# Tile 1 of x loaded from GpSimd's queue, and K's fourth block of weights loaded from ScalarE's queue in its place

## The chip, the cores and the metric

The kernel runs on one core of one Trainium2 chip. The metric is the device time of one execution in microseconds (us); smaller is better. The kernel before takes 210.59 us (median of 3 runs, 210.23 to 210.78).

The engines are named as the profile names them: PE is TensorE (PEld its weight loads), DVE is VectorE, ACT is ScalarE, POOL is GpSimd and SP is SyncE, which here only issues DMAs. A name with a q behind it (SPq, ACTq) is the instruction stream of that engine where it issues a DMA.

## The reference

The input x has 2048 rows of 512 (bfloat16). It is normalised row by row, and two blocks are computed from the normalised rows and added to x:

```python
x  = A_x
xn = _layernorm(x, axis=-1)              # (x - mean) / sqrt(var + 1e-5)
return x + _A_ref(xn, A_wqkv, A_wo) + _B_ref(xn, B_w_gate, B_w_up, B_w_down)
# A: linear attention, 32 heads of 16; phi(t) = where(t > 0, t + 1, exp(t)) + 1e-6
#    q, k, v = xn @ wqkv; kv = phi(k)^T v, z = sum phi(k); out = (phi(q) kv) / (phi(q) z) @ wo
# B: (silu(xn @ w_gate) * (xn @ w_up)) @ w_down, hidden width 1792
```

## The kernel before

The rows are cut into 16 tiles of 128. A tile of x is a 128 KB load; a block of weights of K is 128 rows by 512 columns of `wqkv`, also 128 KB, and a projection of one tile needs four such blocks (0 to 3), one for each 128 of the 512 input features.

Nothing schedules the kernel: every operation is written into the list of one engine in the order of the source, and a small helper (`_Prog`) adds waits on semaphores by what each operation reads and writes. A DMA is one instruction in the list of the engine whose queue issues it, with a semaphore of its own. The helper's rules matter here: an operation that writes a tile waits for the last writer and for all the readers since, and a DMA that is given a tile in `after` counts as a reader of it until it has landed.

The start of the kernel is a chain through all engines, since there is nothing to multiply until the first tile of x has come in:

- PE first runs eight matmuls on constants (`fill(8, 512)`, L271), whose result nobody reads.
- SP issues, in this order: tile 0 of x, blocks 0 and 1 of K's weights (one DMA of 256 KB), block 2 of K's weights, tile 2 of x, two blocks of Q's weights, tile 3 of x, and so on.
- ACT issues two loads before its first work on data: tile 1 of x, which waits for the memset of `ident`, and then block 3 of K's weights, which waits for nothing.
- POOL clears `warm`, clears `ident` (L238), turns `ident` into the identity matrix by an affine select (L242) and sets `nhalf`. Because the load of tile 1 was given `ident` in `after`, the affine select waits until that load has landed.
- Tile 0: DVE takes mean and variance (L299, L302) and subtracts the mean in two halves (L382); PE transposes the halves with `ident` (L410); ACT copies them to `xcT` (L422).
- Tile 1: its mean is taken on ACT instead (`mean_act`, L307); then DVE, PE and ACT do the same as for tile 0.
- PE's list is: the fill; the transposes of tile 0 (first half, one small fill, second half); the two halves of tile 1; and then the projections (`proj_part`, L465), one matmul each. For tile 0 and K the blocks are taken in the order 0, 1, 3, 2; the same follows for tile 1, and then Q.

From there on come the projections of the other tiles (L452, L438), the sums over rows (L590), the feed-forward block (L785) and the output tiles (L979, L990), all on PE in the order of the source.

Of the kernel before, what the change touches and what calls it, by code (L numbers as in the profile page):

```python
# [109 lines left out]
def bass_parallel_sum__linear_attn_block__swiglu_ffn__prompt_kernel(  # L110
# [13 lines left out]
    pe, act, dve, pool, sp = nc.tensor, nc.scalar, nc.vector, nc.gpsimd, nc.sync  # L124
    bf, f32 = dt.bfloat16, dt.float32

    with contextlib.ExitStack() as es:
        E = es.enter_context

        def sb(name, shape, d=bf):  # L130
            return E(nc.sbuf_tensor(name, [P] + shape, d))
# [12 lines left out]
        ident = sb("ident", [P])  # L144
# [54 lines left out]
        def rows(v, t0, n):  # L199
            if t0 < NLONE:  # L200
                return v[t0 * P:(t0 + n) * P, :].rearrange("(t p) d -> p t d", p=P)
            return v[NLONE * P:, :].rearrange("(p t) d -> p t d", t=NT - NLONE)[:, t0 - NLONE:t0 - NLONE + n, :]

        def xload(eng, h, t0, n, after=()):
            K.dma(
                eng, lambda: h.dma_start(x_sb[:, t0:t0 + n, :], rows(xin, t0, n)),
                r=list(after), w=[("x", t0 + i) for i in range(n)],
            )

        def wqkv_load(eng, h, name, i, c0, n, after=()):  # L210
            K.dma(
                eng,
                lambda: h.dma_start(
                    wqkv_sb[:, c0:c0 + n, i * D:(i + 1) * D],
                    A_wqkv[c0 * P:(c0 + n) * P, i * D:(i + 1) * D].rearrange("(c p) f -> p c f", p=P),
                ),
                r=list(after), w=[(name, c) for c in range(c0, c0 + n)],
            )
# [14 lines left out]
            )  # L233

        K.op("pool", lambda: pool.memset(warm[:, :], 0.0), w=[("warm",)])
        K.op("act", lambda: act.activation(warm[:, :], warm[:, :], ACT.Exp), r=[("warm",)], w=[("warm",)])

        K.op("pool", lambda: pool.memset(ident[:, :], 0.0), w=[("ident",)])  # L238
        xload("act", act, 1, 1, [("ident",)])
        K.op(  # L240
            "pool",
            lambda: pool.affine_select(  # L242
# [6 lines left out]

        xload("sp", sp, 0, 1)  # L250
        wqkv_load("sp", sp, "wk", 1, 0, 2)
        wqkv_load("act", act, "wk", 1, 3, 1)
        wqkv_load("sp", sp, "wk", 1, 2, 1)
        xload("sp", sp, 2, 1)
        wqkv_load("sp", sp, "wq", 0, 0, 1)
# [832 lines left out]
```

## Time and profile before

| | us |
|---|---|
| time, median of 3 runs | 210.59 (210.23 to 210.78) |
| the profiled execution's own time | 210.51 |
| its span, first to last instruction | 209.3 |
| outside the span | 1.2 |
| PE busy | 206.6 (99%) |
| DVE, ACT, POOL busy | 120.2, 70.9, 72.0 |

In the profile, times are from the start of the span. A row of the timeline has the start, the length, the engine, the line, the operation, its tiles and how many instructions it merges; in brackets stands how long the engine was idle before it, and what released it. A row of the chain of waits has the start, the length and what ran. In a list of DMA issues the last number is the median time from issue to landing. Matmuls are pipelined: one of 512 columns is shown for about 0.38 us, but the next can start 0.22 us after it.

### The profile page before, as it was taken

The page shows a single profiled execution, that of the slowest core. Times are in us where ns is not written, and L with a number is a line of the kernel's source. Part 1 is how long each engine was busy: PE and PEld are TensorE (multiplying, and loading weights), DVE is VectorE, ACT ScalarE, POOL GpSimd, SP SyncE. Part 2 cuts the span into 40 slices and gives each one's busy share as a digit, 9 for nine tenths or more (in the row PEclk, how much of TensorE's full clock was granted, in tenths as well). Part 3 has the DMA queues.
Part 4 walks back from the last instruction along what each step waited for, and adds up shares of the span by engine and source line. Part 5 has one row for each costly group of instructions (what it writes and reads, how often), then busy time and mean ns, then how long its engine had stood idle before and what let it go on. Part 6 is the DMA issues. An engine that isn't in the chain of part 4 may idle for free.

```text
span 209.3 us, 2824 instructions
## 1 busy us (share of the span) xinstructions
PE 206.6 (99%) x1015; PEld 94.6 (45%) x1015; DVE 120.2 (57%) x246; ACT 70.9 (34%) x125; POOL 72.0 (34%) x90
## 2 busy tenths in 40 slices
PE   8999999999999999999999999999999999999996
PEld 3444444444444444444444444444444444444444
DVE  3999988336365874637355746365556545374122
ACT  5777666966643331312112312213031213121000
POOL 3427977568032543223041422240424132221200
PEclk9999999999999999999999999999999999999999
DMA  6673644894797011010101110102011010110101
GB/s 200 209 195 75 127 100 100 256 364 158 202 357 50 11 39 25 28 25 25 50 2 50 28 29 22 50 0 53 6 45 25 27 28 25 49 30 25 50 28 50
DMA packets 30287, 16.84 MB, mean 80 GB/s; under 512 B 20928, under 2 KB 29632, under 8 KB 30272
## 3 DMA queue, kind: packets, MB, share of 16 engines
q1 hardware_dynamic: 29984, 16.39, 29.9%
q10 hardware_dynamic: 288, 0.26, 0.4%
q8 instruction: 8, 0.13, 0.2%
q14 instruction: 7, 0.06, 0.1%
HBM read 9.70 MB, written 2.10 MB: 56 GB/s over the span
## 4 chain that ended last, share of the span: by engine, by line
PE 99%; DVE 0%; issue 0%
PE psum L785 46%; PE psum L990 23%; PE psum L438 10%; PE psum L979 7%; PE psum L590 7%; PE psum L271 2%; PE psum L465 2%; PE psum L452 2%; PE psum L410 1%; PE psum L892 0%; PE psum L915 0%; DVE out_sb L1003 0%
## 5 line engine op out<-in xcount | busy, mean ns | idle before, releaser
L800 ACT ACTIVATE sg<-psum 128x512 bf16<-128x512 f32 x56 | 33.4, 598 | 106.0 <-PE psum L785 102.5
L785 PE MATMUL psum<-xnT,wg_sb 128*128 128x512 bf16 x224 | 57.5, 379 | 0.0
L785 PE MATMUL psum<-xnT,wu_sb 128*128 128x512 bf16 x224 | 57.5, 379 | 0.0
L934 POOL TENSOR_TENSOR prod<-pkq,zb 128x512 f32<-128x512 bf16 x16 | 18.6, 1163 | 55.9 <-DVE pkq L514 55.9
L785 PEld LDWEIGHTS psum<-xnT,wu_sb 128*128 128x128 bf16 x224 | 21.9, 98 | 26.4
L785 PEld LDWEIGHTS psum<-xnT,wg_sb 128*128 128x128 bf16 x224 | 21.8, 98 | 26.2 <-issue 0.2
L1003 DVE TENSOR_TENSOR out_sb<-psum,x_sb 128x512 bf16<-128x512 f32 (+2 forms) x17 | 11.2, 660 | 35.9 <-PE psum L990 35.9
L958 POOL TENSOR_TENSOR pqn<-pkq,rden 128x512 bf16<-128x512 bf16 x16 | 16.9, 1056 | 36.5 <-DVE rden L952 36.5
L806 DVE TENSOR_TENSOR pkq<-psum,sg 128x512 bf16<-128x512 f32 x28 | 19.2, 686 | 17.1 <-PE psum L785 14.7
L806 DVE TENSOR_TENSOR xn_sb<-psum,sg 128x512 bf16<-128x512 f32 x28 | 18.8, 673 | 14.1 <-PE psum L785 13.6
L990 PE MATMUL psum<-wd_sb,xn_sb 128*128 128x512 bf16 (+2 forms) x126 | 25.7, 355 | 0.0
L990 PE MATMUL psum<-wd_sb,pkq 128*128 128x512 bf16 x112 | 25.5, 379 | 0.0
L438 PE MATMUL psum<-wqkv_sb,xnT 128*128 128x512 bf16 x96 | 22.5, 379 | 0.0
L582 POOL TENSOR_TENSOR zacc<-zacc,pkq 128x512 f32<-128x512 f32 x15 | 17.3, 1155 | 5.0 <-DVE ek L505 4.6
L990 PEld LDWEIGHTS psum<-wd_sb,xn_sb 128*128 128x128 bf16 x126 | 11.8, 98 | 12.5
L990 PEld LDWEIGHTS psum<-wd_sb,pkq 128*128 128x128 bf16 x112 | 11.0, 98 | 13.2
L979 PE MATMUL psum<-m_sb,eq 128*128 128x512 bf16 (+2 forms) x68 | 16.6, 366 | 0.0
L590 PE MATMUL psum<-pkq,xn_sb 128*128 128x512 bf16 x64 | 15.9, 379 | 0.0
L438 PEld LDWEIGHTS psum<-wqkv_sb,xnT 128*128 128x128 bf16 x96 | 9.4, 98 | 11.3
L942 DVE TENSOR_REDUCE den<-prod 128x32 f32<-128x512 f32 x16 | 10.9, 683 | 5.9 <-POOL prod L934 5.9
L299 DVE BATCH_NORM_STATS2 stats<-x_sb 128x6 f32<-128x512 bf16 x16 | 10.9, 681 | 3.4 <-DMA x_sb<-in_A_x_dram 3.4
L514 DVE SCALAR_TENSOR_TENSOR pkq<-pkq,eq 128x512 bf16<-128x512 bf16 x16 | 11.1, 692 | 0.6
(68 smaller groups left out, 138.7 us busy)
## 6 DMA issues: line engine op xcount, KB each, us to landing
out_dram<-out_sb SPq DMA_DIRECT2D x15, 128.0 KB, 1.7
wg_sb<-in_B_w_gate_dram SPq DMA_DIRECT2D x2, 896.0 KB, 7.8
wu_sb<-in_B_w_up_dram SPq DMA_DIRECT2D x2, 896.0 KB, 6.1
wd_sb<-in_B_w_down_dram SPq DMA_DIRECT2D x1, 1792.0 KB, 11.1
x_sb<-in_A_x_dram SPq DMA_DIRECT2D x5, 256.0 KB, 3.1
x_sb<-in_A_x_dram SPq DMA_DIRECT2D x5, 128.0 KB, 3.4
wqkv_sb<-in_A_wqkv_dram SPq DMA_DIRECT2D x5, 128.0 KB, 3.8
wqkv_sb<-in_A_wqkv_dram SPq DMA_DIRECT2D x1, 512.0 KB, 7.9
```

The costliest lines, as they stand in the source:

```text
L438: (lambda c=c: pe.matmul(banks[b], xnT[:, c, t * P:(t + 1) * P], wqkv_sb[:, c, lo:lo + D], start=(c == 0), stop=(c == NDC - 1),))
L514: lambda: dve.scalar_tensor_tensor(out=dst, in0=src, scalar=0.0, in1=e, op0=ALU.max, op1=ALU.add,),
L582: lambda: pool.tensor_tensor(out=zacc[:, :], in0=zacc[:, :], in1=pk, op=ALU.add),
L590: (lambda c=c: pe.matmul(banks[4 + c], xn_sb[:, t, c * P:(c + 1) * P], pkq[:, t, 0, :], start=(t == 0), stop=(t == NT - 1),))
L785: (lambda c=c: pe.matmul(banks[b], w_sb[:, c, fc * P:(fc + 1) * P], xnT[:, c, C * 512:(C + 1) * 512], start=(c == 0), stop=(c == NDC - 1),))
L800: lambda: act.activation(sg[:, j % NSG, :], banks[gb], ACT.Silu),
L806: lambda: dve.tensor_tensor(out=hT(C, fc), in0=banks[ub], in1=sg[:, j % NSG, :], op=ALU.mult,),
L934: lambda: pool.tensor_tensor(out=p, in0=pkq[:, t, 1, :], in1=zb[:, :], op=ALU.mult),
L958: lambda: pool.tensor_tensor(out=pqn[:, t % NPN, :].rearrange("p (i g h e) -> p g i h e", i=NB, g=NG, e=DH), in0=pkq[:, t, 1, :].rearrange ...
L979: (lambda g=g: pe.matmul(dst, pqnT(t)[:, g, :], m_sb[:, g, lo:hi], start=(g == 0), stop=False,))
L990: (lambda fc=fc: pe.matmul(dst, hT(C, fc)[:, jj * P:(jj + 1) * P], wd_sb[:, fc, lo:hi], start=False, stop=(fc == NFC - 1),))
L1003: lambda: dve.tensor_tensor(out=o, in0=src, in1=x_sb[:, t, lo:hi], op=ALU.add),
```

## The change

The load of tile 1 of x goes from ACT's list to POOL's. It stands right behind the memset of `warm` and ahead of the memset of `ident`, and waits for nothing. The load of K's block 3 stays in ACT's list, where it is now the only load, and is given `ident` in `after`. At that place in the source `ident` was last written by the affine select, so that the load now waits for the affine select; and the affine select no longer waits for any load. The instructions of PE, DVE and SP are the same, in the same order.

```diff
         K.op("pool", lambda: pool.memset(warm[:, :], 0.0), w=[("warm",)])
+        xload("pool", pool, 1, 1)
         K.op("act", lambda: act.activation(warm[:, :], warm[:, :], ACT.Exp), r=[("warm",)], w=[("warm",)])

         K.op("pool", lambda: pool.memset(ident[:, :], 0.0), w=[("ident",)])
-        xload("act", act, 1, 1, [("ident",)])
         K.op(
             "pool",
             lambda: pool.affine_select(
...
         wqkv_load("sp", sp, "wk", 1, 0, 2)
-        wqkv_load("act", act, "wk", 1, 3, 1)
+        wqkv_load("act", act, "wk", 1, 3, 1, [("ident",)])
         wqkv_load("sp", sp, "wk", 1, 2, 1)
```

## The prediction

> **What bounds the kernel now.** I read the first and fourth parts of the page, then the chain in order of time, and then the timeline of the first 9 us.
>
> ```profile
> PE 206.6 (99%) x1015; PEld 94.6 (45%) x1015; DVE 120.2 (57%) x246; ACT 70.9 (34%) x125; POOL 72.0 (34%) x90
> PE psum L785 46%; PE psum L990 23%; PE psum L438 10%; PE psum L979 7%; PE psum L590 7%; PE psum L271 2%; PE psum L465 2%; PE psum L452 2%; PE psum L410 1%; PE psum L892 0%; PE psum L915 0%; DVE out_sb L1003 0%
> ```
>
> PE is busy 99% of the span and the whole chain lies on it. Whether it ever waits must be read from its pace:
>
> ```profile
> 0.84 3.57 PE psum L271 x8
> ...
> 5.51 2.75 PE psum L465 x12
> ...
> 8.48 0.86 PE psum L465 x4
> ...
> 55.34 24.28 PE psum L785 x112
> ```
>
> The 112 matmuls of L785 take 24.28 us, 0.217 us each; the four of L465 at 8.48 take 0.86, 0.215 each. The twelve of L465 at 5.51 take 2.75, where 12 x 0.215 would be 2.58: some 0.17 us of waiting is in there. The eight of the fill take 0.45 each: PE starts slow. So PE has a start, and from about 6 us a run at full pace. Any change of the moment where that run begins moves the end by the same amount; nothing after it needs to be costed. This change touches only the start:
>
> ```profile
> 0.80 0.39 SPq L206 DMA_DIRECT2D x_sb<-in_A_x_dram  x1
> 0.83 0.20 POOL L238 MEMSET ident<- 128x128 bf16 x1
> 1.07 0.38 ACTq L206 DMA_DIRECT2D x_sb<-in_A_x_dram  x1
> 1.25 0.93 SPq L213 DMA_DIRECT2D wqkv_sb<-in_A_wqkv_dram  x2
> 1.48 0.45 ACTq L213 DMA_DIRECT2D wqkv_sb<-in_A_wqkv_dram  x1
> 3.37 0.63 ACT L307 ACTIVATE scr<-x_sb 128x512 bf16<-128x512 bf16 x1 [1.08 <-DMA x_sb<-in_A_x_dram]
> 3.57 0.29 POOL L242 TENSOR_SCALAR_AFFINE_SELECT ident<-ident 128x128 bf16<-128x128 bf16 x1 [2.54 <-DMA x_sb<-in_A_x_dram]
> 3.91 0.19 ACT L307 ACTIVATION_READ_ACCUMULATOR scr<-x_sb 128x1 f32 x1
> 4.37 0.40 PE L410 MATMUL psum<-ident,xc_sb 128*128 128x128 bf16 x2
> 4.42 0.48 DVE L382 TENSOR_SCALAR xc_sb<-x_sb,mact 128x256 bf16<-128x256 bf16 x2
> 4.67 0.85 PE L410 MATMUL psum<-ident,xc_sb 128*128 128x128 bf16 x6
> 4.80 1.25 ACT L422 ACTIVATE xcT<-psum 128x256 bf16<-128x256 bf16 x4 [0.71 <-PE psum L410]
> 5.31 2.96 PE L465 MATMUL psum<-wqkv_sb,xcT 128*128 128x512 bf16 x12
> 5.91 1.85 PEld L465 LDWEIGHTS psum<-wqkv_sb,xcT 128*128 128x128 bf16 x10 [0.45 <-ACT xcT L422]
> ```
>
> The two middle issues are the two that change places. The last row is the wait that counts: the weight load of the third L465, which multiplies K's block 3, sat 0.45 us. The profile names ACT's copy, but the half it needs is the second of the four at 4.80 (1.25 / 4 = 0.31 apart), long done. The other thing it waits for is block 3 itself:
>
> ```profile
> x_sb<-in_A_x_dram ACTq DMA_DIRECT2D x1, 128.0 KB, 2.3
> wqkv_sb<-in_A_wqkv_dram ACTq DMA_DIRECT2D x1, 128.0 KB, 4.3
> ```
>
> Issued at 1.48, landed 4.3 later, at 5.8; PE went on at 5.91, 0.11 later. So the transfer that this change delays is already the one that lets PE's run begin. From a narrow look at the same place:
>
> ```profile
> 5.58 0.95 PE L465 MATMUL psum<-wqkv_sb,xcT 128*128 128x512 bf16 x3
> ...
> L465 PE MATMUL psum<-wqkv_sb,xcT x16: 376/379/441, 5.3 to 9.0; 128*128 128x512 bf16 x16
> ...
> wqkv_sb<-in_A_wqkv_dram SPq DMA_DIRECT2D x1, 128.0 KB, 4.3
> ```
>
> The three matmuls end at 6.53; at 0.38 each and 0.215 apart, the middle one, block 3's, starts at 5.94. Without its wait it could have started 0.215 behind 5.58, at 5.80: only 0.14 us is to be had. The last row is block 2's load on SP (the second issue in the row at 1.25, so at 1.72): it lands at 6.0, and its matmul comes next, so it guards nearly the same moment.
>
> **Part 1: POOL's new order.** GpSimd first issues the load (its time is g), then clears `ident` (0.20), then does the affine select (0.29, and in the row at 3.57 it began 0.20 after what it waited for had landed at 1.07 + 2.3 = 3.37). Then ACT issues block 3, with the 0.04 that ACT took before (memset ended 1.03, issue at 1.07): 0.83 + g + 0.20 + 0.20 + 0.29 + 0.04 = 1.56 + g, against 1.48. No row shows a DMA issued by POOL. From below, the hardware queues' issue takes 0.38 (rows at 0.80 and 1.07). From above:
>
> ```profile
> L934 POOL TENSOR_TENSOR prod<-pkq,zb 128x512 f32<-128x512 bf16 x16 | 18.6, 1163 | 55.9 <-DVE pkq L514 55.9
> ...
> 4.08 0.32 POOL L327 TENSOR_SCALAR vpe<-mv 128x1 f32<-128x1 f32 x1 [0.17 <-DVE mv L302]
> ...
> 17.98 0.23 POOL L327 TENSOR_SCALAR vpe<-mv 128x1 f32<-128x1 f32 x1 [0.26 <-DVE mv L302]
> ```
>
> POOL's longest operation is 1.16 us, and its first of a kind can be slower than a later one by 0.32 / 0.23, so 1.6. I take g = 1.4, between 1.16 and 1.6, since it would be the first of its kind there; ends 0.4 and 1.6. The Trainium skill (DMA: Bandwidth & Descriptors, Specifications) gives a first byte after about 1 us on GpSimd's path against 0.6 on SP's and ACT's; as an estimate from that page g would be 0.38 + 0.4 = 0.8, and the sum below would be 0.6 us smaller, which puts block 3 off the path altogether. No row here tests it.
>
> `ident` is then whole at 1.52 + 1.4 = 2.9 instead of 3.86; PE's first transpose waits at 4.37 for DVE, so this gains nothing, and loses nothing while g is below 2.8.
>
> **Part 2: block 3's way from issue to landing, L.** On ACT's queue (q10; packets, MB, share), in three windows, 2 to 3, 3.1 to 4.6 and 4.6 to 5.6 us, and over the whole span:
>
> ```profile
> q10 hardware_dynamic: 143, 0.13, 37.7%
> ...
> q10 hardware_dynamic: 131, 0.12, 25.4%
> ...
> q10 hardware_dynamic: 13, 0.01, 3.0%
> ...
> q10 hardware_dynamic: 288, 0.26, 0.4%
> ```
>
> The 288 packets are two loads of the same size, 144 each. Tile 1's came about 1 us after its issue, within 1 us, and it landed 0.35 later. Block 3's could not begin before tile 1's were through, at 3.0 to 3.1; 131 came by 4.6, and the last 13 dribbled in over another 1 us. In the changed kernel the queue is empty when block 3 is issued, so 1 us to the first packet, then between 1.0 (as tile 1) and 2.5 (as before), then 0.35: L lies between 2.3 and 3.9, and 4.3 as an outer bound if the whole delay was its own. I take the middle, 1 + 1.75 + 0.35 = 3.1.
>
> PE's delay is then (1.56 + g + L + 0.11) - 5.91 = g + L - 4.24 = 1.4 + 3.1 - 4.24 = **+0.26 us**. Ends: 0.4 + 2.3 gives -1.5, which is cut at -0.14 by the 0.215 pace, and at about -0.1 if block 2 lands no earlier; 1.6 + 4.3 gives +1.66.
>
> **Part 3: tile 1's way.** The load starts when its issue is through: 0.83 + g, and then 2.3 - 0.38 = 1.9 (tile 1 before, less its issue). At g = 1.4 it lands at 4.13 instead of 3.37. Behind it: ACT's mean 0.73 (3.37 to 4.10), DVE's two halves with a hand-over 0.51, a hand-over 0.05 and two transposes (0.21 at the start's pace) before the first L465, so 1.50; block 3's matmul two slots (0.44) later: 4.13 + 1.94 = 6.07. Block 3 lets that matmul start at 5.94 + 0.26 = 6.20, so tile 1's 0.76 us is hidden, with 0.13 to spare. Without that cover it would cost g - 1.27. Its bounds: as early as 0.83 + 0.4 + 1.9 = 3.1; as late as 0.83 + 1.6 + 3.0 = 5.4, with the 3.4 less 0.4 of
>
> ```profile
> x_sb<-in_A_x_dram SPq DMA_DIRECT2D x5, 128.0 KB, 3.4
> ...
> 6.24 0.69 DVE L299 BATCH_NORM_STATS2 stats<-x_sb 128x6 f32<-128x512 bf16 x1 [0.33 <-DMA x_sb<-in_A_x_dram]
> ```
>
> which would give +1.4. Queued behind tile 1 on ACT are the copies of tile 0: the mean ends at 4.86 instead of 4.10, 0.06 past 4.80, which the cover takes too. Queued behind it on DVE are the statistics of later tiles; DVE idles 0.33 before tile 2's (last row), so 0.33 of the 0.47 that tile 1's halves come later (4.86 + 0.03 against 4.42) is absorbed there and the rest lies under PE's own delay. SP's queue keeps its order; it has the machine to itself while ACT's load waits, and block 2 may land somewhat earlier. That gives at most the 0.14 above.
>
> **Sum.** The profiled execution took 210.51: a span of 209.3 and 1.2 around it. It becomes 210.77; the median of 210.59 is 0.08 higher, so 210.85, given as **210.9 us**. 0.3%, about what a measurement of this kernel can tell from no change, is 0.63 us.
>
> **The rivals.**
>
> *Block 3 drops off the path.* With g near 0.8 and L near 2.5, g + L is 3.3 and it lands before it is needed; block 2 and the pace bind: -0.14 to +0.05, so 210.5. For it: tile 1 on the same queue took 2.3. Against it: block 3's own load took 4.3. Chance 0.17.
>
> *Block 3 dribbles as long as before.* L = 4.3 and g = 1.4 give +1.46: 212.1, slower. It decides from L above 3.5 (g + L above 4.87). For it: the tail of 13 packets came while SP's queue alone filled the DMA engines, and it still does. Against: much of the 4.3 was time behind tile 1. Chance 0.17.
>
> *POOL's issue is slow.* At g = 2.5 the path through block 3 gives 2.5 + 3.1 - 4.24 = +1.36 and the one through tile 1 gives 2.5 - 1.27 = +1.23, together 212.0, slower; from g = 1.8 it is over 0.3%. For it: all of POOL's preparation now stands behind that issue. Against: nothing on POOL before took over 1.2 us. Chance 0.19.
>
> *POOL has to fetch the code of its first DMA.* With 6 us added, g = 7.4, the path through tile 1 gives +6.1: 216.7. The row at 3.57, where the affine select follows 0.20 after its release, shows no such fetch, so chance 0.05. The Trainium skill (GPSIMD Engine Reference, 2.1 Instruction dispatch) has this price: about 6 us at the first call of a freshly loaded kernel.
>
> *Faster by over 0.63 us.* PE's pace allows 0.14; more would need the early matmuls at full speed sooner, which nothing here moves. Chance 0.04.
>
> **How the numbers follow.** The forecast, +0.05 to +0.63, has 0.38; with the first rival, 0.55 for within 0.3%. The other three mechanisms that cost time make 0.41, and 0.04 is left for faster. The range goes from 210.3 (the first rival, and as much again for what the three runs differ) to 212.1 (block 3's dribble and POOL's issue): it leaves out the code fetch and the worse halves of those two. The forecast and the first rival alone would span 210.3 to 211.3.
>
> **What would show it.** Right: a POOL issue row of 1.2 to 1.6 at 0.83, the affine select ending near 2.9, ACT's issue of block 3 near 3.0, landing near 6.1, the third weight load of L465 near 6.2, and the same 0.217 pace afterwards. The first step is wrong if POOL's row is under 1 or over 2 us; the second if block 3 takes under 2.7 or over 3.6 to land; the third if PE's transposes of tile 1, not block 3, are the last thing before L465. The whole is wrong if PE's pace has gaps later than 7 us, or if the end moves by another amount than the start of PE's run.

## The result

The changed kernel is slower: 211.62 us (median of 9 runs, 211.10 to 213.08) against 210.31 us for the kernel before, measured beside it (9 runs, 210.07 to 211.01). The ratio of the runs, which is not that of the medians, is 1.0075, with a 95% interval of 1.0057 to 1.0092: a loss of 0.75%. Between the medians alone it is 1.31 us, 0.62%.

The nine runs fall in two groups: five at 211.10 to 211.62 and four at 212.84 to 213.08. The profile first taken of the change is of the lower group (211.34, a span of 210.1). Two more profiles of the same kernel, below, fell in the upper one, and the two groups have different causes of loss.

### The profile page after: what moved, and what is told of

Read it like the earlier page. It is cut to its first block, busy times and chain, and to the rows that moved or that the text cites. A ratio compares the mean times of both kernels' runs of the same rounds, so it can differ in the third digit from the quotient of the medians.

```text
span 210.1 us, 2804 instructions
## 1 busy us (share of the span) xinstructions
PE 205.4 (98%) x996; PEld 94.2 (45%) x1015; DVE 120.3 (57%) x246; ACT 70.8 (34%) x125; POOL 72.7 (35%) x91
## 4 chain that ended last, share of the span: by engine, by line
PE 96%; DMA 2%; issue 1%; ACT 0%; DVE 0%; POOL 0%; POOLq 0%
PE psum L785 46%; PE psum L990 23%; PE psum L438 10%; PE psum L979 7%; PE psum L590 7%; PE psum L465 2%; PE psum L452 2%; DMA x_sb<-in_A_x_dram 2%; ACT scr L307 0%; PE psum L410 0%; PE psum L892 0%; PE psum L915 0%; DVE xc_sb L382 0%; DVE out_sb L1003 0%; POOL warm L235 0%
## 5 line engine op out<-in xcount | busy, mean ns | idle before, releaser
L785 PE MATMUL psum<-xnT,wu_sb 128*128 128x512 bf16 x216 | 55.8, 379 | 0.4
L990 PEld LDWEIGHTS psum<-wd_sb,xn_sb 128*128 128x128 bf16 x126 | 11.8, 98 | 12.5
```

What stands on the lines that cost most here:

```text
L785: (lambda c=c: pe.matmul(banks[b], w_sb[:, c, fc * P:(fc + 1) * P], xnT[:, c, C * 512:(C + 1) * 512], start=(c == 0), stop=(c == NDC - 1),))
L990: (lambda fc=fc: pe.matmul(dst, hT(C, fc)[:, jj * P:(jj + 1) * P], wd_sb[:, fc, lo:hi], start=False, stop=(fc == NFC - 1),))
```

## The profile after

The chain of waits of the changed kernel from the start to the end of PE's first twelve projections (start, length, what):

```profile
1.33 3.38 DMA x_sb<-in_A_x_dram
...
4.73 0.73 ACT scr L307 x2
...
5.49 0.30 DVE xc_sb L382
...
5.83 0.48 PE psum L410 x4
6.32 0.43 PE psum L465 x2
6.75 0.03 issue
6.77 2.32 PE psum L465 x10
```

Before, the chain of this stretch lay on PE from 0.84 on. Now 3.4 us of it, up to 4.71, are the load of tile 1 from GpSimd's queue. The twelve L465 end at 6.77 + 2.32 = 9.09; before they ended at 5.51 + 2.75 = 8.26. The difference is 0.83 us, and the profiled executions differ by 211.34 - 210.51 = 0.83. So in this run everything happened ahead of 9.1 us, and the rest of the kernel follows at its old pace.

From the timeline of the same stretch, the rows that answer to those of before:

```profile
1.33 0.77 POOL L206 DMA_DIRECT2D x_sb<-in_A_x_dram  x1 [0.43 <-issue]
2.10 0.23 POOL L239 MEMSET ident<- 128x128 bf16 x1
2.58 0.29 POOL L242 TENSOR_SCALAR_AFFINE_SELECT ident<-ident 128x128 bf16<-128x128 bf16 x1 [0.24 <-POOL ident L239]
2.90 0.39 ACTq L213 DMA_DIRECT2D wqkv_sb<-in_A_wqkv_dram  x1
4.73 0.63 ACT L307 ACTIVATE scr<-x_sb 128x512 bf16<-128x512 bf16 x1 [2.44 <-DMA x_sb<-in_A_x_dram]
5.83 0.48 PE L410 MATMUL psum<-ident,xc_sb 128*128 128x128 bf16 x4 [0.85 <-DVE xc_sb L382]
6.74 0.78 PEld L465 LDWEIGHTS psum<-wqkv_sb,xcT 128*128 128x128 bf16 x5 [0.49 <-ACT xcT L422]
```

and the two loads that changed places (last number: us from issue to landing):

```profile
x_sb<-in_A_x_dram POOLq DMA_DIRECT2D x1, 128.0 KB, 3.4
wqkv_sb<-in_A_wqkv_dram ACTq DMA_DIRECT2D x1, 128.0 KB, 3.7
```

Tile 1 lands at 1.33 + 3.4 = 4.7 (3.37 before), block 3 at 2.90 + 3.7 = 6.6 (5.8 before). Two waits stand on PE's way. Ahead of tile 1's transposes PE is idle, 0.85 us by the row at 5.83 and nearer 1.0 if the pipelined ends are taken off. Then the third L465 waits for block 3: its weight load is at 6.74 instead of 5.91, which is the 0.83. The profile again names ACT's copy there, which was done before block 3 landed at 6.6.

The upper group, in the chain of the third profile of the same kernel (213.07 us), with its two loads:

```profile
6.40 4.42 PE psum L465 x12
```

```profile
x_sb<-in_A_x_dram POOLq DMA_DIRECT2D x1, 128.0 KB, 3.3
wqkv_sb<-in_A_wqkv_dram ACTq DMA_DIRECT2D x1, 128.0 KB, 3.8
```

The loads are as in the lower run. The twelve L465 take 4.42 us instead of 2.75: at 0.43 each while PE runs at its starting pace and 0.215 afterwards, (4.42 - 12 x 0.215) / 0.215 = 8.6, so eight or nine of them ran at the starting pace. They end at 10.82, 2.56 after the 8.26 of before, and the executions differ by 213.07 - 210.51 = 2.56. Of this, 6.40 - 5.51 = 0.89 is the later start behind tile 1's transposes, and 4.42 - 2.75 = 1.67 is the pace. At this pace the third L465 comes two slots of 0.43 behind the first, later than block 3 lets it, so block 3 costs nothing here.

## Experiments

The theories after this profile were these. **A**: two loads lead to the third L465, and the later one alone decides. **C**: PE's idle stretch ahead of tile 1's transposes lets its clock (the speed at which it takes matmuls, read here from their spacing) come up later in some runs; that makes the upper group. **D**, about why block 3 took 3.7 us and not 3.1 or less: it waits behind what was issued before it. **E**, its rival, came later: it is stretched by what is issued after it.

### Block 3 early: tile 1's path alone

```diff
-        wqkv_load("act", act, "wk", 1, 3, 1, [("ident",)])
+        wqkv_load("act", act, "wk", 1, 3, 1)
```

(against the changed kernel, as all that follow where nothing else is said)

> Tile 1 of x stays on GpSimd's queue, but block 3 goes out on ScalarE's queue at once, at about 0.8 us, with no wait. Theory A (two paths, the later one decides: in the profiled run of the change block 3 landed at 6.64 and tile 1 at 4.71): block 3 lands before 5, and only tile 1's path is left: lands near 4.7, third L465 at 4.71 + 1.87 = 6.58 instead of 5.94 before, so +0.64 us of span against before. Rival B (all of the profiled run's loss is block 3's, tile 1 is hidden): within 0.15 us of before. Theory C (the change's nine runs fall in two groups, 211.1 to 211.6 and 212.8 to 213.1, because PE stands idle for about 1 us ahead of tile 1's transposes, and in some runs its clock then comes up one step later): the idle is still there, so a part of the runs is again about 1.5 us longer.

Measured: 213.65 us (6 runs: 211.44, 211.71, and four at 213.50 to 214.07), ratio to before 1.0124 (1.0084 to 1.0163). The chain of its profile, of the run at 211.71:

```profile
1.33 3.93 DMA x_sb<-in_A_x_dram
...
6.87 2.59 PE psum L465 x12
```

Block 3 landed at 3.3 and PE never waits for it: 2.59 for the twelve is 12 x 0.216. The loss is there all the same, from tile 1, which landed at 1.33 + 3.93 = 5.26 here. The twelve end at 9.46, 1.20 late, as the run is (211.71 - 210.51). Tile 1's load alone costs, so rival B falls. It cost more than the 0.64 expected, because tile 1 landed 0.55 later than in the change's profile. The upper runs did not go away; they are four of six here.

### Block 3 late: its path alone

```diff
-        xload("pool", pool, 1, 1)
+        xload("act", act, 1, 1)
+        K.op("pool", lambda: pool.memset(prod[:, :, :], 0.0), w=[("prod", 0), ("prod", 1)])
```

> Tile 1 is loaded from ScalarE's queue at once, at 0.8 us; in the place of the load GpSimd clears a 128x1024 buffer of float32 that nothing reads then, so that block 3 is again issued only when GpSimd is done, near 2.9 us. Theory A: tile 1 lands near 3.1, block 3 near 6.6, third L465 near 6.8: +0.8 us of span, the same as the change, since the later path decides and the two do not add. Rival B' (tile 1's landing from GpSimd's queue is what costs): no loss, within 0.2 us of before. Theory C: PE is now idle 0.5 to 0.8 us, and later (5.9 to 6.7), with its clock already up or about to be; fewer runs with the extra 1.5 us than the change has, or none.

Measured: 211.20 us (10 runs, 210.85 to 211.45), ratio 1.0034 (1.0023 to 1.0045). The chain (line numbers are one higher in this kernel):

```profile
2.48 4.14 DMA wqkv_sb<-in_A_wqkv_dram
6.62 0.14 issue
6.76 2.32 PE psum L466 x10
```

Block 3 was issued at 2.48 and landed at 6.62; the third L465 starts at 6.76, as in the change, and the run (211.33) is as late. The exact match is luck: the issue was 0.42 earlier than in the change and the load 0.4 longer. Tile 1 landed at 3.7, not 3.1, which was still early enough. So either load alone makes a loss of this size, and together they make no more: in the lower group the later path decides, as theory A has it. A late tile 1 is not needed for it, so B' falls as the only cause. There is no upper group in ten runs.

### Filling PE's idle stretch

```diff
+        fill(2, 512)
         tp_first(1, 0, 6)
```

> The changed kernel with two more matmuls of 512 columns on constants ahead of the transposes of tile 1, where PE stood idle from 4.78 to 5.83 us; at the start's pace they last 0.85 us. Theory C: PE has no idle stretch left in which its clock could miss a step, the group at 212.8 to 213.1 goes and all runs lie at 211.0 to 211.8: median 0.3 us or more under the change's. Rival (the two groups come from when the loads land): two groups as in the change, median within 0.2 us of the change's 211.6.

Measured: 211.32 us (6 runs, 211.07 to 211.43), ratio 1.004 (1.0026 to 1.0055), below the whole interval of the change. No run of the upper group is left. The profile's PE run begins as late as the change's:

```profile
6.84 2.32 PE psum L465 x10
```

So with two matmuls that compute nothing the upper group is gone from these six runs, and the loads' loss of some 0.9 us is left. That is theory C's expectation; by the rival they could not have helped. The profile itself does not show the two at work: in it the eighth matmul of the fill, at 3.78, is already the last slow one (0.44 us long where the others are 0.63), so the pace had come up ahead of them. The evidence is the six runs, against four upper ones of nine in the change.

### The same idle stretch in the kernel before

```diff
-        fill(8, 512)
+        fill(6, 512)
```

(against the kernel before)

> The kernel before with six matmuls in the fill instead of eight: PE has 0.85 us less to do and stands idle from about 3.4 to 4.37 us; no load and no wait is changed. Theory C: the idle alone makes a second group of runs, up to 1.5 us above the kernel before, and its profile (if of that group) shows L465 starting 0.43 us apart instead of 0.22 for some us. Rival: no change, within 0.2 us of before in every run, since PE waits there anyway.

Measured: seven runs at 210.11 to 210.47 and five at 211.63 to 212.66 (median 210.35), where 21 runs of the kernel before beside them lay between 210.06 and 211.00 (median 210.37); the ratio is 1.0034 (1.0004 to 1.0063). Nothing of the loads was touched; with two matmuls fewer there is an upper group, 1.3 to 2.3 us above that median where up to 1.5 was expected. Its profile is of a lower run, 210.11, so the pace of an upper one wasn't seen here. The chain of that lower run:

```profile
5.18 2.65 PE psum L465 x12
```

The twelve end at 7.83, 0.43 earlier than in the profile of the kernel before, and the run is 0.40 faster than its 210.51. Both the pace (the small fill matmul at 4.43 is 0.22 us long, where it was 0.31) and block 3 (3.9 us instead of 4.3) came earlier in it. So two lower runs can differ by this much with the same loads in the same order.

### Half the fill in the changed kernel

```diff
-        fill(8, 512)
+        fill(4, 512)
```

> The changed kernel with four matmuls in the fill instead of eight: PE stands idle from about 2.5 to 4.3 us and again from 4.7 to 5.8. No load changes. Theory C (idle at the start makes PE's clock come up one step of some 3.4 us later): nearly every run is in the upper group, 212.5 to 214.5, and the profile shows L465 and what follows 0.43 us apart, not 0.22, up to about 9 us; PE's third L465 still starts near 6.8. Rival (the groups come from the landings): two groups or one, but not above the change's 213.1, and 0.22 us pace from 6 us on.

Measured: 213.05 us (4 runs, 212.47 to 213.62), ratio 1.0115 (1.0087 to 1.0142): every run is in the upper group's region. The chain:

```profile
6.18 4.04 PE psum L465 x12
```

The profiled run is 212.47, and the twelve take 4.04 us, much as the 4.42 of the change's third profile. They end at 10.22, 1.96 late; the run is 1.96 late.

### Two more profiles of the change, one more of block 3 early

> A second look at the changed kernel itself, of whose nine runs four were at 212.8 to 213.1. Theory C: a run near 211.4 shows the twelve L465 in about 2.8 us, one near 212.9 shows them in about 4, 0.43 us apart, with tile 1 landing at about 4.7 and block 3 at about 6.6 in both. Rival: the upper runs have one of the two loads 1.5 us later, and the pace is 0.22 in both.

> The same look a third time, since a single execution falls in either group: near 211.4 with the twelve L465 in about 2.8 us, or near 212.9 with them in about 4; by theory C the landings of tile 1 (4.7) and block 3 (6.6) are the same in both.

> A second look at the kernel with block 3 issued early and tile 1 on GpSimd's queue, of whose six runs four were at 213.5 to 214.1 and whose profile was of the lower ones, 211.7. Theory C: if this run is an upper one, its profile shows matmuls 0.43 us apart for a stretch of about 3.4 us after 6 us, and the third L465 starts as in the lower run. Rival: the upper runs are those in which tile 1 lands some 2 us later.

The second profile of the change was of a run of 212.65, the third of 213.07 (shown above), the second of block 3 early of 212.85. The chains of the second profile of the change and of block 3 early:

```profile
6.27 4.13 PE psum L465 x12
```

```profile
1.33 3.50 DMA x_sb<-in_A_x_dram
...
6.56 4.01 PE psum L465 x12
```

All three have the starting pace far into L465. The weight loads of single matmuls in the second profile of the change show it, 0.43 us apart:

```profile
7.35 0.15 PEld L465 LDWEIGHTS psum<-wqkv_sb,xcT 128*128 128x128 bf16 x1 [0.28 <-issue]
7.78 0.15 PEld L465 LDWEIGHTS psum<-wqkv_sb,xcT 128*128 128x128 bf16 x1 [0.28 <-issue]
8.20 0.15 PEld L465 LDWEIGHTS psum<-wqkv_sb,xcT 128*128 128x128 bf16 x1 [0.28 <-issue]
```

Neither of the two loads is later by anything like 1.5 us: in the second profile tile 1 took 3.2 and block 3 3.8 us to land, against 3.4 and 3.7; in block 3 early tile 1 took 3.50 against 3.93 in its lower run. (There tile 0 landed 0.4 later, which moves PE's first transposes and lengthens the idle ahead of them, but not the start of L465, which is earlier than in the lower run.) So the upper group is PE's pace, not the landings.

### Fewer loads ahead of block 3

```diff
-        xload("sp", sp, 2, 1)
+        xload("sp", sp, 2, 1, [("ident",)])
```

> The changed kernel in which SP's fourth load (tile 2 of x) also waits for the affect of the affine select, so that it and all of SP's later loads go out from 2.9 us on, and block 3 stands fifth in the order of issue instead of seventh. Theory D (loads land in the order in which all queues together issued them, so block 3's 3.74 us were the loads ahead of it): block 3 lands 0.7 us or more earlier than in the change's profile, before 5.9; then tile 1 is last and PE's third L465 starts near 6.6 instead of 6.77. Rival (the first load on an idle ScalarE queue takes its 3.7 us whatever else is issued): lands near 6.6 again.

Measured: 211.53 us (5 runs: four at 211.48 to 211.56, one at 212.93), ratio 1.0059 (1.0029 to 1.0089). The loads of tile 2 and of block 3:

```profile
x_sb<-in_A_x_dram SPq DMA_DIRECT2D x1, 128.0 KB, 3.7
wqkv_sb<-in_A_wqkv_dram ACTq DMA_DIRECT2D x1, 128.0 KB, 3.9
```

Block 3 took 3.9 us and landed at 6.8, so theory D's number failed. The edit did less than was planned: SP issued tile 2 at the same 2.90 us, and it landed at 6.6, still ahead of block 3, so that one load fewer was ahead and not two. And SP's other held-back loads followed from 3.3 us on, so this did not show whether the ones behind matter.

### Tile 1 from SP's queue

```diff
-        xload("pool", pool, 1, 1)
+        K.op("pool", lambda: pool.memset(prod[:, :, :], 0.0), w=[("prod", 0), ("prod", 1)])
...
         wqkv_load("sp", sp, "wk", 1, 0, 2)
...
+        xload("sp", sp, 1, 1)
         wqkv_load("sp", sp, "wk", 1, 2, 1)
```

> The changed kernel with tile 1's load taken off GpSimd's queue and put third on SP's, between the two loads of K's blocks, issued near 1.7 us; GpSimd clears a 128x1024 float32 buffer in its place, and block 3 goes out near 2.5 us. Theory D (landing goes by place in the common order, and GpSimd's load was also third): tile 1 lands between 4.3 and 5.3 us, no better than the change's 4.71. Rival S (GpSimd's way of issuing is what made tile 1 late): 2.3 to 2.4 us from issue to landing as for tiles 0 and 1 before, so at 4.1 or earlier. By D block 3, fifth in order, lands before 6.4.

Measured: 211.41 us (7 runs, 211.02 to 211.63), ratio 1.0031 (1.0017 to 1.0044). Tile 1 in its chain:

```profile
1.72 2.70 DMA x_sb<-in_A_x_dram
```

It landed at 4.42, inside D's 4.3 to 5.3 and later than S's 4.1: issued third, tile 1 is late from SP's queue too. From issue to landing it took 2.70 in this one profile, and 3.1 to 3.9 from GpSimd's queue in the nine profiles that had it there, so a share of 0.4 us or more is probably GpSimd's own. D's other number failed: block 3 landed at 6.7, not before 6.4, though it was issued at 2.49, 0.41 earlier than in the change. None of the seven runs is an upper one, although PE is idle ahead of tile 1's transposes here too.

### Nothing behind block 3

```diff
-        xload("sp", sp, 2, 1)
+        xload("sp", sp, 2, 1, [("wk", 3)])
```

> The changed kernel in which SP's load of tile 2, and with it all of SP's later loads, waits until block 3 has landed. It is a measurement of block 3's load with nothing issued behind it, not a candidate: Q's weights and tile 2 come some 3 us late and the time will be 2 us or more longer. Block 3 is issued at 2.9 us behind the same three SP loads and tile 1's. Theory E (what stretches it from 2.3 to 3.7 us is sharing the DMA engines with loads issued after it): lands 2.2 to 2.8 us after its issue, by 5.7. Rival F (it waits behind what was issued before it, or some DMA engine stands still then whatever is issued): 3.5 us or more, past 6.4.

Measured: 212.41 us in one run, 1.4 over the one run of the kernel before beside it (210.99), with Q's weights late as foreseen but less of a loss than the 2 us given. Block 3's load:

```profile
wqkv_sb<-in_A_wqkv_dram ACTq DMA_DIRECT2D x1, 128.0 KB, 2.6
```

It took 2.6 us instead of 3.7, and landed at 5.5; ahead of it were tile 0, tile 1 and blocks 0 to 2, as in "Fewer loads ahead of block 3", where SP's other loads went out with it and after it and it took 3.9. Theory E's number came true, in one profile: what lengthens block 3's load is the loads that SP goes on to issue. From 4.50 to 5.47 us the DMA engines were busy 0.29 of the time here, and 0.91 there.

### The kernel before, with the later loads held back

The last finding points to a better kernel: let SP wait with tile 2 and all behind it until tile 1 is there.

```diff
-        xload("sp", sp, 2, 1)
+        xload("sp", sp, 2, 1, [("x", 1)])
```

(against the kernel before)

> The kernel before, in which SP's load of tile 2, and so all of SP's later loads, waits until tile 1 has landed (3.35 us before); nothing else is changed. Theory E (a load is stretched by those issued after it): blocks 3 and 2 land by 5.2 instead of 5.8 and 6.0, tile 2 and Q's blocks no later than before (6.2, 6.5, 6.9), PE's third L465 no longer waits and starts at 5.8 or earlier: 0.1 to 0.4 us of span gained, faster by 0.05 to 0.2%. Rival: the hole in the landings near 5 us stays, or tile 2 and Q's first block come later than before and PE waits for them at 7.2 us: no gain, or up to 0.5 us lost.

Measured: 210.76 us (12 runs, 210.60 to 210.92), ratio 1.0019 (1.0010 to 1.0028): a small loss. Block 3's load, and the chain:

```profile
wqkv_sb<-in_A_wqkv_dram ACTq DMA_DIRECT2D x1, 128.0 KB, 3.4
```

```profile
5.47 2.83 PE psum L465 x12
...
11.98 0.12 issue
```

The first half came true: block 3 took 3.4 us instead of 4.3 (3.9 in the profile with six fill matmuls, whose loads are those of before) and landed at 4.9, block 2 at 5.1. The third L465 still starts at 5.98, not 5.8, and the twelve end at 8.30, because the first of them ran at PE's starting pace (2.83 us for the twelve, though block 3 was there), and the held-back loads turn up later as a new wait. In the timeline of this kernel SP's transpose of tile 3, and the weight load that needs it:

```profile
9.26 1.28 SPq L401 DMA_TRANSPOSE xcT<-xc_sb  x1
...
11.86 0.56 PEld L452 LDWEIGHTS psum<-wqkv_sb,xcT 128*128 128x128 bf16 x4 [0.37 <-ACT kpos L528]
```

That transpose was issued at 8.96 before, and at a landing time of 2.5 us it comes in at 11.8, just ahead of the weight load. In this profile the two make 0.11 us, 210.62 against 210.51; the rest of the 0.39 between the medians was not traced. None of the kernels tried is clear of noise faster than the kernel before.

## Why the prediction was right or wrong

The forecast was a small loss, within 0.3%; the measured loss is 0.75% over all runs and 0.62% between the medians, inside the stated range and beyond what was given as the likeliest. The direction, and block 3 as what binds, were right for the lower group. That the median lies inside the range is in part luck: it is the highest of the five lower runs, the four upper ones (212.84 and more) lie above the range's end of 212.1, and one more of them would have put the median there. Of the 1.31 us between the medians, 0.83 is what the two profiles explain; 211.62 is 0.28 above the profiled run of the change, and 210.31 is 0.20 below that of the kernel before. By its steps:

- **PE's run and what it costs to start it later** held in every profile where the loads behind it came in time: the end of the twelve L465, taken against 8.26, gave the whole run's difference to 0.05 us (0.83 for the change, 1.20, 1.96 and 2.56 above). What it lacked is that the start has a length as well as a moment: the matmuls of L465 were all taken at 0.215 each. In the upper group the end moves by more than the start of L465 does (2.56 against 0.89 in the third profile), which the forecast had named as a sign that the whole is wrong.
- **Part 1, POOL's order**, was right in its sum, and not in how the sum is made up. g was taken as 1.4; POOL's issue ended at 2.10, 1.27 after 0.83. The affine select ended at 2.87 (2.9 forecast) and ACT issued at 2.90 (2.96). But the issue row is 0.77 long and starts at 1.33, behind 0.43 of idle, where a row of 1.2 to 1.6 at 0.83 was forecast and one under 1 was to be the sign of a wrong step. The 1.4 came from POOL's longest operation, which is other work, so that it came close is partly luck. The Trainium skill's first-byte figures (DMA: Bandwidth & Descriptors, Specifications), from which 0.8 was estimated, fit worse here: the measured 1.27 decides.
- **Part 2, L**, is the term of the sum that was mis-sized: 3.7 measured for the 3.1 taken, from a range of 2.3 to 3.9. This is the gap between the +0.26 forecast and the +0.83 of the lower run: 0.6 more for the load, less 0.06 for the earlier issue. By the forecast's own sign, over 3.6 us, this is the step that failed. It was reasoned from the load's own queue, which would be empty; the runs showed that the other queue counts, 2.6 us without later loads and 3.7 with them. The Trainium skill says as much (DMA: Bandwidth & Descriptors, Issuing engines are not separate DMA queues: loads issued by several engines run on the same 16 DMA engines and interleave), and the 2.6 and 3.7 agree. The row for five of SP's own loads of weights stood in the page before (shown below the list) and would have been the better neighbour.
- **Part 3, tile 1's way**: it landed at 4.71, not 4.13, since it took 2.6 us and not 1.9 from the end of its issue. That it is hidden behind block 3 held in the lower run, with about 0.2 to spare; taken alone it costs as much or more, as the first experiment showed. In the upper runs it is not hidden, since there the slow matmuls behind it are later than block 3.
- **The rivals.** Block 3's dribble as long as before (L = 4.3, +1.46) had the mechanism, at nearly twice the size. POOL did not fetch code, and its issue was not over 1.6. The sentence that failed was in the last rival, that nothing here moves the early matmuls' pace: the change does move it, the wrong way. A rival was missing, PE idle for about 1 us in the stretch where its pace has yet to come up, and as far as the runs show it is what makes four runs of nine some 1.4 us longer.
- **What would show it**: the forecast asked for PE's pace behind the start to be the same. It is in the lower group; in the upper one it is not up to 9 us.

```profile
wqkv_sb<-in_A_wqkv_dram SPq DMA_DIRECT2D x5, 128.0 KB, 3.8
```

## What to carry to other kernels

Where one engine runs without a gap from its start to the end, read how its start is timed and at which pace, and not only which wait ends last there: an idle stretch of a microsecond on PE ahead of its first real work can cost more than the load it waited for, and matmuls that compute nothing were a cheap cover here. Price a load by the loads that run beside it on all queues, not by its own queue. Measure such a change more than once: one profile showed 0.83 us, and four runs of nine had lost 2.3 us and more.

## What the runs showed of the hardware

- PE's pace at the start is 0.43 us for a matmul of 512 columns and 0.215 later, and the moment of the switch differs between runs of one kernel: before the first L465 in the change's first profile, past 9 us in its second and third, with the two loads landing within 0.2 us of the same times. Read from the single matmuls of all fourteen profiles, the switch is over by 6.8 us in ten, and lies between 8.9 and 10 us in the four of upper runs. Idle time makes runs of the upper group more common: no run of the kernel before was above 211.01, five of twelve with 0.85 us less fill were, and all four with half the fill and the change's idle stretch. The length of the idle stretch does not decide it in a single run: ahead of tile 1's transposes it is 1.36 us in the lower run of block 3 early, and 0.61 in the second profile of the change, an upper run. What else does was not tested. The Trainium skill (TensorE: Matmul & The Clock Gate, Part 1) describes a window of about 3.4 us that runs freely and must be busy before the clock comes up; the two groups and what fills and gaps do to them agree. No run here shows the window itself.
- The profile's granted clock does not show this. In the stretches of the change (length, PE busy, clock, DMA share, GB/s) both rows have 1.00, the second with all eight fill matmuls 0.43 us apart; the pace of the matmuls has to be read instead:

```profile
4.78:5.82 1.04, 0.20 (x2) 1.00 0.95 326
0.84:4.20 3.36, 3.36 (x8) 1.00 0.66 176
```

- A load from GpSimd's queue stood 0.77 us on POOL, with 0.43 of idle ahead of it, and took 3.1 to 3.9 us from issue to landing in nine profiles; one from SP's queue, also third in the order of issue, took 2.7 in the one profile that has it.
- Left open: why the landings have a hole in them. Before, blocks 0 and 1 landed at 4.15 and the next load, block 3, at 5.8; in the change block 3 landed at 6.6 after a stretch in which the DMA engines were busy for 0.95 (first row above). Loads issued later explain that block 3 is stretched (2.6 us alone); why it comes in one step of over a microsecond was not found. Nor was why block 3 lands at 6.6 to 6.8 in every kernel that issues it late with SP's loads going on, whether it is issued at 2.48 or at 2.90.
